# One visit instead of two for the softmax sums of the last head pair, at the seam between attention and a routed MLP

## The chip, the cores and the metric

The kernel runs on one core of one Trainium2 chip. The metric is the device time of one execution in microseconds (us), the median of three runs. A profiled execution of the same kernel gives the trace from which all durations below come.

## What is computed

The reference, cut to what matters. Attention in which a query sees only the keys of its own cluster, then a router that sends each token to one of eight experts:

```python
q_assign = argmax(q_n @ c_n.T)              # 16 clusters per head; k_assign likewise
mask = q_assign[..., :, None] == k_assign[..., None, :]
attn = softmax(where(mask, (q @ k.T) / 8, -1e9))        # B=4, H=8, S=768, D=64
x = (attn @ v).transpose(0, 2, 1, 3).reshape(3072, 512)
logits = unit(x) @ unit(expert_emb).T / tau              # 8 experts
expert_idx = argmax(logits); gate = softmax(logits)[expert_idx]
out[n] = gate[n] * (relu(x[n] @ w1[e]) @ w2[e])          # e = expert_idx[n], F=1024
```

Everything is float32.

## The kernel before

**Attention.** There are 16 pairs of heads, numbered n = 0 to 15: four to each batch, so that n = 12 to 15 make up batch 3. Each pair is cut into two groups of queries (hq = 0, 1; group g = 2n + hq) and each group into six tiles of 128 keys. One turn of the main loop (from L1547) treats two such units; a pair has turns it = 0 to 5, of which 0 to 2 belong to the first group and 3 to 5 to the second. In a turn TensorE (PE) makes the scores of the next turn (`scores`, L557), ScalarE (ACT) takes their exponentials (`expo`, L568), PE multiplies the previous ones with v (`attend`, L579), and VectorE (DVE) adds the exponentials up in `acc` (L588, L598).

**Dividing.** `total` (L617) sums `acc` over the partitions with a matmul against ones (L629). For an inner pair it is called once for both groups, one turn into the next pair: 8 matmuls of 32 x 192, then on DVE a transpose and a reciprocal of 12 values to a row (L646, L647), then eight small copies on GpSimd (POOL, L650) into `inv2`; two turns later `divide` (L654) spreads them by a DVE transpose (L661) and multiplies (L665). For the last pair it is called once for each group, each with 2 matmuls of 64 x 384 and a DVE reciprocal of 384 values to a row (L638): group 30 at turn 3, group 31 behind attention. `rows` (L676) transposes the result (L682) and writes it to the internal DRAM tensor x_rows (L689, four DMAs on the queue of SyncE, SP). `route_pieces` holds the router: `products` (L708) multiplies x with the expert vectors, in one visit for both groups of a batch or, in batch 3, once for each; `logits` (L720), `choose` (L756 to L763), `read` (L730, L735) and `norms` (L741) follow.

**The MLP.** The order of work on every engine is written out by hand; a scheduler reorders nothing, and each engine runs its queue in order. Four early items E0[0] to E0[3], each of 128 tokens of batches 0 and 1, are treated while the last routing is still being worked out. `spread_rows` sends their token numbers through DRAM (L1098, L1100), and `spread_pieces` turns them into addresses (two DVE instructions, L1106 and L1107). `early_lot(j, n)` issues the next n of the four indirect gathers of item j on POOL (L1130), optionally behind a copy of one element, `pace` (L1460), which makes POOL wait for a tile of ACT. `turn_x` transposes the gathered rows (L1248 on DVE; for E0[0] on PE, L1255, and ACT, L1258). `hidden` multiplies with w1 (L1372) in two halves of 512 columns, each followed by a relu on ACT (L1379); `result` multiplies with w2 (L1412) and ACT scales by the gate (L1423). `weights1` and `weights2` load 2 MB each on SP (L1180).

**The routing chain.** With all batches chosen, `pb.ranks` counts on PE (L844, L851). DVE then runs one long chain: `firsts`, `dest`, `hot_blocks` (L1007, L1011; L1010 on POOL) and `hot_rows` (L1017), after which PE makes `tokens` (L1026). `pieces` (L1115 on PE, L1123 on DVE) gives the addresses for the later items. From there PE alternates hidden and result of blocks and "sized" items (L1279, L1317) until the end.

Of the kernel before, what the change touches and what calls it, by code (L numbers as in the profile page):

```python
# [9 lines left out]
F32 = mybir.dt.float32  # L10
# [3 lines left out]
ACTF = mybir.ActivationFunctionType  # L14
AXX = mybir.AxisListType.X
EngineType = mybir.EngineType
PSUM = bass.MemoryType.PSUM

P = 128

SQ = 32
# [13 lines left out]
def bc(ap, shape, axis):  # L35
    return ap.unsqueeze(axis).to_broadcast(shape)
# [3 lines left out]
def kernel(  # L40
# [576 lines left out]
    def total(*gs):  # L617

        g = gs[0]
        d = gr[g]  # L620
        n = units[GU * g][0]
        G = len(gs)
        bk = misc()

        M, W = (D, HS) if G == 1 else (D // 2, HS // 2)
        for i in range(P // M):
            for k, g in enumerate(gs):
                c = i * W % HS
                nc.tensor.matmul(  # L629
                    bk[M * i : M * i + M, W * k : W * k + W],  # L630
                    lhsT=ones[:, 0:M],
                    rhs=gr[g]["acc"][:, i * W // HS, c : c + W],
                    start=True,
                    stop=True,
                )
        den = d["den"] = smp.tile([P, G, HS], F32, tag="den", name="den", bufs=1)
        if G == 1:
            nc.vector.reciprocal(den[:, 0], bk[:, 0:W])  # L638
            return


        U = W // SQ
        sums = smp.tile([P, G * U, SQ], F32, tag="sums", name="sums", bufs=1)
        inv = smp.tile([P, G, U], F32, tag="inv", name="inv", bufs=1)
        inv2 = d["inv2"] = smp.tile([P, G, 2, U], F32, tag="inv2", name="inv2", bufs=1)
        nc.vector.transpose(sums.rearrange("p g i -> p (g i)"), bk[:, 0 : G * W])  # L646
        nc.vector.reciprocal(inv.rearrange("p k u -> p (k u)"), sums[:, :, 0])  # L647
        for i in range(4):
            for to in (i, i ^ 1):
                nc.gpsimd.tensor_copy(  # L650
                    inv2[M * to : M * to + M, :, i % 2], inv[M * i : M * i + M]
                )

    def divide(*gs):  # L654
        n, hq, _ = units[GU * gs[0]]
        d = gr[gs[0]]
        G = len(gs)
        if hq == 0:
            xT[pairs[n]] = xp.tile([P, 2, HS], F32, tag="xT", name="xT", bufs=4)
        if G == 2:  # L660
            nc.vector.transpose(  # L661
                d["den"].rearrange("p k (u t) -> p (k u) t", t=SQ),
                bc(d["inv2"].rearrange("p k h u -> p (k h u)"), [P, G * HS // SQ, SQ], 2),
            )
        nc.vector.scalar_tensor_tensor(  # L665
            out=xT[pairs[n]][:, hq : hq + G],
            in0=ld[n]["o_sum"][:, hq : hq + G, 0:HS],
            scalar=ld[n]["o_sum"][:, hq, HS:HE],
            in1=d["den"],
            op0=ALU.add,  # L670
            op1=ALU.mult,
        )
        for g in gs:
            gr[g].clear()

    def rows(*gs):  # L676

        n, hq, _ = units[GU * gs[0]]
        b, hp = pairs[n]
        G = len(gs)  # L680
        xb = smp.tile([P, G * HS // SQ, SQ], F32, tag="xb", name="xb", bufs=2)
        nc.vector.transpose(  # L682
            xb.rearrange("p g i -> p (g i)"),
            xT[b, hp][:, hq : hq + G].rearrange("p k t -> p (k t)"),
        )
        t0 = S * b + HS * hq
        for c in range(P // SQ):
            c0 = P * c + SQ * hp
            nc.sync.dma_start(  # L689
                out=x_rows[t0 : t0 + G * HS, c0 : c0 + SQ].rearrange("(g t) i -> t g i", t=SQ),  # L690
                in_=xb[SQ * c : SQ * c + SQ],
            )
# [533 lines left out]
    def order_x(it):  # L1226

        d = mo[it]
        d["rows"] = xip.tile([P, KD, NQ, SQ], F32, tag="rows", name="rows")
        nc.gpsimd.tensor_copy(d["rows"], d["xin"].rearrange("p w (c i) -> p c w i", i=SQ))  # L1230
# [124 lines left out]
    def flat(t):  # L1355
        return t.rearrange("p k w -> p (k w)")

    def hidden(it, halves=(0, 1)):

        d = mo[it]  # L1360
        for half in halves:
            if half == 0:
                d["hT"] = (
                    flat(szp.tile([P, KF, max(CAPS)], F32, tag="hTs", name="hTs", bufs=1))[:, 0:F]
                    if it.kind == "whole"
                    else mop.tile([P, F], F32, tag="hT", name="hT")
                )
            f0 = 512 * half
            bk = psH.tile([P, 512], F32, tag="h_ps", name="h_ps")
            for m in range(0, 512, P):  # L1370
                for c in range(KD):
                    nc.tensor.matmul(  # L1372
                        bk[:, m : m + P],
                        lhsT=w1s[it.slot][:, c, f0 + m : f0 + m + P],
                        rhs=d["xT"][:, P * c : P * c + P],
                        start=(c == 0),
                        stop=(c == KD - 1),
                    )
            nc.scalar.activation(d["hT"][:, f0 : f0 + 512], bk, ACTF.Relu)  # L1379

    def result_last(it):

# [18 lines left out]
    def result(it, halves=(0, 1)):  # L1401
# [42 lines left out]
            pa.spread_rows(),  # L1444
        ),
        (3, 2, 3): lambda: fetch(E0[0]),
        (3, 2, 5): lambda: (order_x(E0[0]), pa.spread_pieces()),
        (3, 3, 2): lambda: early_lot(1, 2),
        (3, 3, 3): lambda: early_lot(1, 1),
        (3, 3, 4): lambda: early_lot(1, 1),  # L1450
# [94 lines left out]
    with tc.manual_schedule(engines=by_hand):  # L1545
        begin()
        for i in range(0, len(units), 2):  # L1547
            n, it = divmod(i // 2, NJ)

            if n == it == 0:  # L1550
                load(2, "qk")
            if it == 2 and n + 1 < NP:
                load(n + 1, "v")
            if it >= 4 and n + 3 < NP:
                load(n + 3, "qk"[it - 4])
            for m in range(i + 2 if i else 4, min(i + 4, len(units))):
                scores(m)
                expo(m)
                if it == 2 and m == i + 2:
                    piece(n + 1, "codes")  # L1560
            if (n, it) == (0, 1):
                piece(1, "products")
            between(n, it)
            if it == 4 and n == NP - 1:
                divide(2 * n)
            b, nb = divmod(n, NHP)
            if (b, nb, it) in early:
                early[b, nb, it]()
            if it >= 4:
                piece(n + 2, f"turn{it - 4}")  # L1570
            if i + 2 == len(units):
                ats.close()
                tile_waits = {"side": "right", "reuse_waits": "tile"}
                psX = ctx.enter_context(tc.tile_pool(name="psX", bufs=1, space=PSUM, **tile_waits))
                turn_x(E0[0], nc.scalar.copy, xp.tile([P, DM], F32, tag="acc", name="xTm", bufs=3))
            for m in range(i, i + 2):
                attend(m)
                if m == 0:
                    scores(3, (1,))
                    scores(3, (0,))  # L1580
                    expo(3)
            if it == 2:
                if n > 0:
                    divide(2 * n - 2, 2 * n - 1)
                unite(2 * n)
            elif it == 5:
                unite(2 * n + 1)
            if i + 2 == len(units):
                rows(ngroups - 2)
                route[b][0](0)  # L1590
            if it == 0 and n > 0:
                total(2 * n - 2, 2 * n - 1)
            if it == 0 and n > 0:
                piece(n + 1, "products")
            if (nb, it) == (0, 4) and b > 0:
                route[b - 1][0](0, 1)
            if it == 3 and n == NP - 1:
                total(2 * n)
        at.close()
        mop = ctx.enter_context(tc.tile_pool(name="mop", bufs=2, **tile_waits))  # L1600
        rtb = ctx.enter_context(tc.tile_pool(name="rtb", bufs=1, **tile_waits))
# [9 lines left out]
        gates = gate_pieces(0, B - 1)  # L1611
        gates[0]()
        early_lot(2, 1)
        logits(0)
        hidden(E0[0], (0,))
        turn_x(E0[1])
        early_lot(2, 2, mo[E0[0]]["hT"][0:1, 511:512])
        total(ngroups - 1)
        divide(ngroups - 1)
        ato.close()  # L1620
        psY = ctx.enter_context(tc.tile_pool(name="psY", bufs=1, space=PSUM, reuse_waits="tile"))
        rows(ngroups - 1)
        gates[1]()
        gates[2]()
        hidden(E0[0], (1,))
        turn_x(E0[2])
        gates[3]()
        early_lot(3, 2, mo[E0[0]]["hT"][0:1, F - 1 : F])
        weights1(E0[2])
        read(0, NJ, P - SQ, P)  # L1630
        products(1)
        hidden(E0[1], (0,))
        logits(1)
        choose()
        early_lot(3, 2, mo[E0[1]]["hT"][0:1, 511:512])
        hidden(E0[1], (1,))
        weights1(E0[3])
        pb.ranks()
# [8 lines left out]
        pb.hot_blocks()  # L1647
        pb.hot_rows(0, 1)
        hidden(E0[2])
        pb.experts()  # L1650
        weights1(later[0])
        result(E0[1], (0,))
# [186 lines left out]
```

## Time and profile before

| quantity | value |
|---|---|
| median of three runs | 695.13 us (694.39 to 695.2) |
| the profiled execution's own time | 691.63 us |
| its span, first to last instruction | 689.8 us |
| PE busy in the span | 680.6 us, 99% |
| DVE / POOL / ACT busy | 383.7 / 274.5 / 262.7 us |
| granted clock of PE | 0.998 |
| first router product behind attention (L708) | 323.69 us |
| first matmul of E0[3] | 362.94 us |

The profile is read as follows. A line of the timeline has the start in us from the start of the span, the length in us, the engine, the source line, the operation, what it writes and reads, the shape, and the count of merged instructions; brackets give the idle time of the engine before it and what ended it. A float32 matmul shows as two records. A busy PE says only that some matmul was in flight.

### The profile page before, as it was taken

Reading aid. Unit: us, or ns where it says so; the run is one execution under the profiler, and the core shown is the slowest. Engines: PE = TensorE matmul, PEld = TensorE weight load, DVE = VectorE, ACT = ScalarE, POOL = GpSimd, SP = SyncE. Lnnn points to the kernel's source line nnn. Section 1 sums busy time; section 2 is a strip of 40 time slices with the busy share of each in tenths; the row PEclk is TensorE's granted clock in tenths of the full one; section 3 lists DMA queues with packets and bytes.
Section 4 is the critical chain, followed back from the end, with each engine's and each line's share of the span. In section 5 each row is a group of like instructions: output and inputs, shape, how many; then the busy total and the mean of one; then the engine's idle time right before and its main releaser. Section 6 shows DMA issues by size and latency. Waiting matters only on the chain.

```text
span 689.8 us, 16335 instructions
## 1 busy us (share of the span) xinstructions
PE 680.6 (99%) x6521; PEld 459.6 (67%) x6521; DVE 383.7 (56%) x673; ACT 262.7 (38%) x444; POOL 274.5 (40%) x507
## 2 busy tenths in 40 slices
PE   8999999999999999999999999999999999999997
PEld 4444444444444444445866678888979797979795
DVE  6889898998889999979674122140210303030310
ACT  6666565577656765566242120101010111111011
POOL 3222221321132221326526343576746464647403
PEclk9999999999999999999999999999999999999999
DMA  9656665875677677789799967357777676878640
GB/s 152 118 81 113 106 98 85 161 143 102 107 132 158 114 153 159 182 204 255 205 323 395 354 221 271 120 201 281 287 244 284 213 288 249 304 257 305 234 169 34
DMA packets 244989, 135.55 MB, mean 196 GB/s; under 512 B 208673, under 2 KB 208675, under 8 KB 244909
## 3 DMA queue, kind: packets, MB, share of 16 engines
q1 hardware_dynamic: 237740, 121.09, 65.6%
q0 software_dynamic: 6224, 13.14, 5.6%
q8 instruction: 53, 0.87, 0.5%
q10 hardware_dynamic: 944, 0.23, 0.1%
q14 instruction: 28, 0.22, 0.1%
HBM read 115.93 MB, written 13.12 MB: 187 GB/s over the span
## 4 chain that ended last, share of the span: by engine, by line
PE 80%; DVE 7%; issue 5%; DMA 5%; POOL 1%; ACT 1%; POOLq 0%; SPq 0%; DVEq 0%; ACTq 0%
PE s_ps L557 17%; PE o_ps L579 14%; PE h_ps L1372 10%; PE y_ps L1412 10%; PE h_ps L1279 9%; PE y_ps L1317 6%; PE misc L1317 5%; PE x_ps L1279 3%; DVE acc L598 3%; DMA out_dram<-ys,spidx 2%; PE misc L629 2%; DMA w1s<-in_moe_w_dram 1%; PE misc L418 1%; PE misc L708 1%; POOL out_dram L1141 1%
## 5 line engine op out<-in xcount | busy, mean ns | idle before, releaser
L568 ACT ACTIVATE prob<-s_ps 128x768 f32<-128x768 f32 x192 | 154.4, 814 | 102.1 <-PE s_ps L557 101.2
L557 PE MATMUL s_ps<-qT,kT 64*64 64x384 f32 x1536 | 156.0, 483 | 0.0
L579 PE MATMUL o_ps<-prob,v 64*64 64x385 f32 x1536 | 141.2, 484 | 0.0
L598 DVE TENSOR_TENSOR acc<-acc,prob 128x768 f32<-128x768 f32 x128 | 121.3, 948 | 8.8 <-ACT prob L568 0.5
L579 PEld LDWEIGHTS o_ps<-prob,v 64*64 64x64 f32 x1536 | 58.1, 133 | 64.8 <-issue 56.8
L1326 DVE STREAM_TRANSPOSE ys<-y_ps 128x256 f32<-128x256 f32 (+4 forms) x16 | 6.5, 412 | 147.7 <-PE y_ps L1317 147.7
L1372 PEld LDWEIGHTS h_ps<-xTm,w1s 128*128 128x128 f32 x768 | 87.3, 192 | 2.0 <-issue 1.5
L1372 PE MATMUL h_ps<-xTm,w1s 128*128 128x128 f32 x768 | 88.3, 276 | 0.0
L557 PEld LDWEIGHTS s_ps<-qT,kT 64*64 64x64 f32 x1536 | 55.3, 133 | 36.3 <-issue 32.4
L1412 PE MATMUL y_ps<-w2s,hT 128*128 128x512 f32 x176 | 77.8, 594 | 0.4 <-PEq L1720 0.4
L613 POOL COPY behind<-acc 1x1 f32<-1x1 f32 x30 | 6.7, 222 | 172.3 <-DVE acc L598 167.9
L1279 PE MATMUL h_ps<-xTs,w1s 128*128 128x272 f32 (+7 forms) x384 | 72.8, 346 | 0.0
L1279 PEld LDWEIGHTS h_ps<-xTs,w1s 128*128 128x128 f32 x384 | 66.7, 190 | 6.6 <-issue 2.9
L1141 POOL DMA_INDIRECT out_dram<-ys,spidx x56 | 56.2, 1004 | 36.4 <-issue 20.0
L1379 ACT ACTIVATE hT<-h_ps 128x512 f32<-128x512 f32 x24 | 14.3, 596 | 143.7 <-PE h_ps L1372 143.6
L557 PE MATMUL s_ps<-hot 64*64 64x384 bf16 x768 | 64.4, 325 | 0.6 <-ACT hot L511 0.6
L1130 POOL DMA_INDIRECT xs<-x_rows,gpidx x56 | 56.9, 1017 | 18.1 <-issue 17.2
L1412 PEld LDWEIGHTS y_ps<-w2s,hT 128*128 128x128 f32 x176 | 32.5, 190 | 37.5 <-issue 37.5
L557 PEld LDWEIGHTS <-hot 64*64 64x64 bf16 x768 | 23.9, 106 | 43.1 <-issue 41.2
L1317 PE MATMUL y_ps<-hTs,w2o 128*128 128x272 f32 (+7 forms) x256 | 48.0, 346 | 0.0
L1317 PE MATMUL misc<-hTs,w2o 128*128 128x272 f32 (+7 forms) x256 | 48.0, 346 | 0.0
L1317 PEld LDWEIGHTS y_ps<-hTs,w2o 128*128 128x128 f32 x256 | 44.4, 190 | 2.5
(288 smaller groups left out, 728.7 us busy)
## 6 DMA issues: line engine op xcount, KB each, us to landing
w1s<-in_moe_w_dram SPq DMA_DIRECT2D x18, 2048.0 KB, 8.6
w2s<-in_moe_w_dram SPq DMA_DIRECT2D x18, 2048.0 KB, 10.0
q<-in_q_dram SPq DMA_DIRECT2D x63, 96.0 KB, 3.9
k<-in_k_dram SPq DMA_DIRECT2D x63, 96.0 KB, 3.5
v<-in_v_dram SPq DMA_DIRECT2D x120, 48.0 KB, 2.1
x_rows<-xb SPq DMA_DIRECT2D x60, 96.0 KB, 2.7
xr<-x_rows SPq DMA_DIRECT2D x9, 512.0 KB, 4.5
w1s<-in_moe_w_dram SPq DMA_DIRECT2D x4, 1024.0 KB
```

What stands on the lines that cost most here:

```text
L557: nc.tensor.matmul(s_ps[D * half : D * half + D, h, 0:HS], lhsT=l[rows, half], rhs=r[rows], start=part == (1 if len(parts) < 2 else 0), st ...
L568: nc.scalar.activation(d["prob"][:, :, 0:HS], d["s_ps"][:, :, 0:HS], ACTF.Exp, scale=scale)
L579: nc.tensor.matmul(g["o_ps"][D * h : D * h + D, half, 0:HE], lhsT=ld[n]["v"][keys, j, h], rhs=d["prob"][keys, h, 0:HE], start=(j == 0), st ...
L598: nc.vector.tensor_tensor(g["acc"], g["acc"], d["prob"][:, :, 0:HS], ALU.add)
L629: nc.tensor.matmul(bk[M * i : M * i + M, W * k : W * k + W], lhsT=ones[:, 0:M], rhs=gr[g]["acc"][:, i * W // HS, c : c + W], start=True, s ...
L1130: nc.gpsimd.indirect_dma_start(out=to, out_offset=None, in_=of, in_offset=bass.IndirectOffsetOnAxis(ap=at, axis=0), bounds_check=n - 1, oo ...
L1141: inst = nc.gpsimd.indirect_dma_start(out=to, out_offset=bass.IndirectOffsetOnAxis(ap=at, axis=0), in_=of, in_offset=None, bounds_check=n - 1,
L1279: nc.tensor.matmul(bk, lhsT=w1s[it.slot][:, c, P * f : P * f + P], rhs=d["xT"][:, c, 0:C], start=(c == 0), stop=(c == KD - 1),)
L1317: nc.tensor.matmul(bks[g][:, 0:C], lhsT=d["w2"][:, f, P * g : P * g + P], rhs=d["hT"][:, f, 0:C], start=(f == 0), stop=(f == KF - 1),)
L1372: nc.tensor.matmul(bk[:, m : m + P], lhsT=w1s[it.slot][:, c, f0 + m : f0 + m + P], rhs=d["xT"][:, P * c : P * c + P], start=(c == 0), stop ...
L1379: nc.scalar.activation(d["hT"][:, f0 : f0 + 512], bk, ACTF.Relu)
L1412: nc.tensor.matmul(bk, lhsT=d["hT"][:, P * c : P * c + P], rhs=w2s[it.slot][:, c], start=(c == 0), stop=(c == KF - 1),)
```

## The change

Three things are edited, and the order of the seam with them.

1. `total` and `divide` lose their one-group form. The calls for group 30 at turns 3 and 4 of pair 15 go; groups 30 and 31 are summed, divided and written together behind attention. The router's products of batch 3 are likewise made in one visit (`products(0, 1)`), set between two quarters of E0[1]'s hidden layer: `hidden` gets a `span` for that.
2. `spread_pieces` moves from turn 5 of pair 14 to turn 1 of pair 15.
3. Behind attention, E0[1]'s transpose, the gate steps of the first three batches (`gates[1]` to `gates[3]`) and the load of w1 for E0[2] move ahead of the divide and of the x_rows writes; E0[2]'s transpose moves behind `choose`; the gathers of E0[3] move: one stays early, two are paced by the first half of E0[2]'s hidden layer and the last by its second half.

```diff
         (3, 2, 3): lambda: fetch(E0[0]),
-        (3, 2, 5): lambda: (order_x(E0[0]), pa.spread_pieces()),
+        (3, 2, 5): lambda: order_x(E0[0]),
+        (3, 3, 1): pa.spread_pieces,
...
-            if it == 4 and n == NP - 1:
-                divide(2 * n)
...
-            if i + 2 == len(units):
-                rows(ngroups - 2)
-                route[b][0](0)
...
-            if it == 3 and n == NP - 1:
-                total(2 * n)
...
         early_lot(2, 1)
-        logits(0)
+        turn_x(E0[1])
         hidden(E0[0], (0,))
-        turn_x(E0[1])
-        early_lot(2, 2, mo[E0[0]]["hT"][0:1, 511:512])
-        total(ngroups - 1)
-        divide(ngroups - 1)
-        ato.close()
-        psY = ctx.enter_context(tc.tile_pool(name="psY", bufs=1, space=PSUM, reuse_waits="tile"))
-        rows(ngroups - 1)
+        total(ngroups - 2, ngroups - 1)
         gates[1]()
         gates[2]()
         hidden(E0[0], (1,))
+        gates[3]()
+        weights1(E0[2])
+        divide(ngroups - 2, ngroups - 1)
+        ato.close()
+        psY = ctx.enter_context(tc.tile_pool(name="psY", bufs=1, space=PSUM, reuse_waits="tile"))
+        rows(ngroups - 2, ngroups - 1)
+        read(0, NJ, P - SQ, P)
+        hidden(E0[1], (0,), (0, 256))
+        products(0, 1)
+        hidden(E0[1], (0,), (256, 512))
+        early_lot(2, 2, mo[E0[0]]["hT"][0:1, F - 1 : F])
+        early_lot(3, 1)
+        logits(0, 1)
+        choose()
         turn_x(E0[2])
-        gates[3]()
-        early_lot(3, 2, mo[E0[0]]["hT"][0:1, F - 1 : F])
-        weights1(E0[2])
-        read(0, NJ, P - SQ, P)
-        products(1)
-        hidden(E0[1], (0,))
-        logits(1)
-        choose()
-        early_lot(3, 2, mo[E0[1]]["hT"][0:1, 511:512])
         hidden(E0[1], (1,))
...
         pb.hot_blocks()
         pb.hot_rows(0, 1)
         hidden(E0[2])
+        early_lot(3, 2, mo[E0[2]]["hT"][0:1, 511:512])
+        early_lot(3, 1, mo[E0[2]]["hT"][0:1, F - 1 : F])
         pb.experts()
```

More of the change, by code (lines that the diff above doesn't have):

```diff
@@ L623, in total @@
         bk = misc()
-        M, W = (D, HS) if G == 1 else (D // 2, HS // 2)
+        M, W = D // 2, HS // 2
         for i in range(P // M):
@@ L635, in total @@
                 )
[L636 to L639, printed above, removed]
+        d["den"] = smp.tile([P, G, HS], F32, tag="den", name="den", bufs=1)
         U = W // SQ
@@ L659, in divide @@
             xT[pairs[n]] = xp.tile([P, 2, HS], F32, tag="xT", name="xT", bufs=4)
[L660 to L664, printed above, removed]
+        nc.vector.transpose(
+            d["den"].rearrange("p k (u t) -> p (k u) t", t=SQ),
+            bc(d["inv2"].rearrange("p k h u -> p (k h u)"), [P, G * HS // SQ, SQ], 2),
+        )
         nc.vector.scalar_tensor_tensor(
@@ L1356, in flat, with hidden @@
         return t.rearrange("p k w -> p (k w)")
-    def hidden(it, halves=(0, 1)):
+    def hidden(it, halves=(0, 1), span=(0, 512)):
         d = mo[it]
         for half in halves:
-            if half == 0:
+            if half == 0 and span[0] == 0:
                 d["hT"] = (
@@ L1368, in hidden @@
             f0 = 512 * half
-            bk = psH.tile([P, 512], F32, tag="h_ps", name="h_ps")
-            for m in range(0, 512, P):
+            if span[0] == 0:
+                d["h_ps"] = psH.tile([P, 512], F32, tag="h_ps", name="h_ps")
+            bk = d["h_ps"]
+            for m in range(*span, P):
                 for c in range(KD):
@@ L1378, in hidden @@
                     )
-            nc.scalar.activation(d["hT"][:, f0 : f0 + 512], bk, ACTF.Relu)
+            if span[1] == 512:
+                nc.scalar.activation(d["hT"][:, f0 : f0 + 512], bk, ACTF.Relu)
     def result_last(it):
```

## The prediction

> **What bounds the kernel.** I read first the busy times, then what PE waited for, then the chain of waits before its one wait.
>
> ```profile
> PE 680.6 (99%) x6521; PEld 459.6 (67%) x6521; DVE 383.7 (56%) x673; ACT 262.7 (38%) x444; POOL 274.5 (40%) x507
> ```
>
> ```profile
> PE misc L629 <- DVE acc L598: 1.1, 1, 1.1
> ```
>
> ```profile
> 302.08 3.55 DMA early_f<-early_rows
> ...
> 305.75 0.25 DVE early_f L1106
> ...
> 308.17 0.88 PE misc L629 x14
> ```
>
> PE is the bound, with one wait of over 0.6 us behind the start: at turn 0 of pair 15 L629 needs group 29's `acc`, DVE holds that back behind L1106, and L1106 waits for the token numbers' DMA. A PE microsecond saved near here counts, unless something else then holds PE. So I priced the PE instructions from start to next start:
>
> ```profile
> 182.17 1.51 PE L708 MATMUL misc<-xT,embT 128*32 128x192 f32 x32
> 183.61 0.36 PE L557 MATMUL s_ps<-hot 64*64 64x384 bf16 x4
> ```
>
> ```profile
> 306.54 0.51 PE L629 MATMUL misc<-acc,ones 128*32 128x192 f32 x2
> 308.17 0.88 PE L629 MATMUL misc<-acc,ones 128*32 128x192 f32 x14 [1.12 <-DVE acc L598]
> 308.98 0.36 PE L557 MATMUL s_ps<-hot 64*64 64x384 bf16 x4
> ```
>
> ```profile
> 328.26 0.87 PE L629 MATMUL misc<-acc,ones 128*64 128x384 f32 x4
> 329.06 3.84 PE L1372 MATMUL h_ps<-xTm,w1s 128*128 128x128 f32 x32
> 332.82 0.87 PE L708 MATMUL misc<-xT,embT 128*32 128x96 f32 x32
> ```
>
> A products visit over both groups takes 1.44 us (182.17 to 183.61); one over half of them 0.80 (332.82 to 333.62, where the next line starts). A single-group total takes 0.80. Last, the engines that decide when the moved gathers go out:
>
> ```profile
> 310.89 4.30 POOL L650 COPY inv<-inv 32x12 f32<-32x12 f32 x8 [1.64 <-DVE inv L647]
> ```
>
> ```profile
> 352.07 4.23 DVE L1017 TENSOR_TENSOR ohrb<-io_b,lob 128x3072 bf16<-128x3072 bf16 x1
> ```
>
> ```profile
> 496.83 1.23 DVE L1341 TENSOR_TENSOR ys<-ys,gates 128x1024 f32<-128x1024 f32 x1
> ```
>
> ```profile
> 496.98 1.96 POOL L1130 DMA_INDIRECT xin<-x_rows,gpidx  x1 [0.30 <-issue]
> ```
>
> Eight L650 copies take 2.23 us at 290.13, but 4.30 here, beside four of DVE's acc additions. The gather at 496.98 takes 1.96 us instead of about 1.0; it ends 0.9 us after L1341 does.
>
> [...] every other copy there (0.80 to 0.82 us, the rest 0.18) ends just behind an addition, and a one-element L613 copy at 25.21 took 0.85 us under such an instruction, 0.18 elsewhere. [...] from issue to landing a gather took 3.0 us in a lull (331.07), 5.6 and 5.8 beside the weight loads (367.97, 369.32), at worst 7.9 (386.36).
>
> **Part by part.**
>
> *`spread_pieces` one turn later.* It issues two DVE instructions and no DMA. Its DMA had landed by 305.65; at the new place, behind L647 (about 308.3), it waits for nothing, and the gathers that need it follow on POOL behind the L650 copies, as before. DVE then ends group 29's `acc` near 304.7, before PE asks at 306.54. PE spent 308.98 - 306.54 = 2.44 us; the sixteen records alone cost 0.68 (286.92 to 287.60, where a like shape follows) to 0.90; I take 0.78. Gain 1.66.
>
> *Group 30's total gone from turn 3.* From `attend` to the next scores: 316.43 to 318.62 = 2.19 us, against 1.30 in the turn before (313.52 to 314.82). Gain 0.89.
>
> *First products gone.* 322.24 to 324.49 = 2.25, against 1.40 for an `attend` followed by a change of shape (320.26 to 321.66). Gain 0.85.
>
> *Joint total*: 0.77 for 0.80. Gain 0.03. *Joint products*: 1.44 for 0.80. Loss 0.64.
>
> PE sum: 1.66 + 0.89 + 0.85 + 0.03 - 0.64 = 2.79 us, bounds 2.5 to 2.95. L844 moves from 340.87 to 338.08.
>
> *New PE wait: the joint products' last four matmuls need pair 15's quotient.* Total ends 325.6; L647's successor 326.5; eight copies 2.23, since DVE has little here: 328.9; transpose and multiply 0.97 + 1.02: 331.0. PE arrives at 332.2. Cost nothing; with the 4.30 us of the row above, 0.7 us. The moved gate steps on DVE (eight small instructions) lie beside the copies. E0[1]'s transpose now stands ahead of the total's transpose and waits for four gathers, issued by about 318, so landed by 324: nothing. Two reciprocals of 2.55 us leave DVE, which isn't the bound: nothing.
>
> *SP.* Eight x_rows DMAs of 48 KB become four of 96 KB and fall behind gate_rows and w1 of E0[2]. That load goes out near 331.8 instead of 338.79 and takes 8.8 us; PE needs it at 345.3 (348.10 - 2.79), so the old 338.79 + 8.8 = 347.6 would have become a stall, and it doesn't. x_rows and the reads behind queue after it and pass about when they did; w1 of E0[3] follows near 347 (was 348.37).
>
> *E0[2]'s transpose ahead of the routing chain.* Its last gather goes out near 332.6 and lands in 5 us beside that load; transposed by 338.4, when L859 is due. Delay of DVE's chain 0 to 0.8; I take 0.15. So L1017 ends at 356.30 - 2.79 + 0.15 = 353.66.
>
> *E0[3]'s gathers: the added wait that decides.* Before, they went out by 341.2. Now three of them stand behind the four gate gathers, a scatter and L1010. POOL takes a `pace` copy when L1010 is done, about 350.4[...]: it ends at 353.7. Queued behind it: gather (1.03), pause 0.31, gather (1.00), the second `pace` (relu done by 353.1), pauses of 0.16: the last gather is issued at 356.6. The DMA engines are then full, w1 and w2 loads of 4 MB from 347 on and the next from 356: 5.5 us to landing, 362.1. DVE transposes in 0.71, with L1123 queued behind: PE can begin E0[3] at 362.9. PE is ready at 362.94 - 2.79 = 360.15. Stall 2.75 us, bounds: nothing (landing within 3.5) to 5.1 (7.9).
>
> From there PE runs as before, from 362.9 against 362.94. All later loads wait for PE or for addresses that come when they came.
>
> **Sum.** -2.79 + 2.75 = about 0. The profiled execution took 691.63 (span 689.8 and 1.8 around it) and lies 3.5 below the median, 695.13; a difference in microseconds carries over. Forecast 695.1; its own range, 694.0 to 696.3, from landings of 4.5 to 6.5. A change of 0.2%, 1.4 us, is about what a measurement of this kernel can tell from none.
>
> **Rivals.**
>
> *The gain stays (0.28).* If POOL's `pace` copy gets in ahead of L1017, the last gather goes out with the relu, near 353.9, lands at 359.4, is turned by 360.2: no stall, 692.3. A landing of 4.1 gives half: 693.7. For it: the first half's relu is done by 349.6, well before L1017 ends, and some gathers needed only 3.0. Against: L1010 stands ahead in POOL's queue[...]; the weights fill the engines.
>
> *Slower (0.14).* The same gather lands late: with 7.9, PE begins E0[3] at 365.3, 2.4 us later than now: 697.5. It decides from a landing of 6.9 us on (stall 4.2). For it: 6.6 to 7.9 stand in the trace. Against: those were the first of their burst, and this is the last.
>
> *The quotient comes late.* Stall of 0.7 at the joint products, which pushes the routing chain as much: 695.8, inside the likeliest case.
>
> *The old stall doesn't go*: L1106's wait would only move. Against: its DMA landed 2.6 us before the new place.
>
> **Chances.** No change 0.58, faster by over 0.2% 0.28, slower 0.14. The range 692.4 to 696.8 leaves out the full gain's lower edge and the late landing, some 0.15.
>
> **What would show it.** Right: no PE wait at L629 at 306.5, L844 near 338.1, one new PE wait of 2 to 3.5 us before L1372 of E0[3], released by DVE's transpose, itself by the gather; a `pace` copy of some 3 us beside L1017. Wrong: that copy at 0.18 us; a last gather before 355; a wait at L708; or L844 later than 338.6.

## The result, and the profile after

| runs of one session | before, us | after, us | after / before (95% interval) |
|---|---|---|---|
| the result | 695.04 (22 runs) | 697.88 (22 runs) | 1.0035 (1.0023 to 1.0047) |
| chip 3 | 691.03 (33) | 696.66 (2) | 1.008 (1.0062 to 1.0099) |
| chip 7 | 695.30 (39) | 700.36 (21) | 1.0062 (1.0048 to 1.0075) |

The change makes the kernel slower: by 2.8 us of the median in the result, by 5.1 to 5.6 in two later sessions. The forecast was 695.1, no change. Chips differ in their base: the kernel before takes a median of 690.9 to 691.0 us on two of them and 695.0 to 695.3 in the other sessions. Medians are set against those of the kernel before from the same session; where profiles of different sessions are compared, the text says so.

The page's busy times after, and the list of what PE waited for (total, times, longest):

```profile
PE 682.8 (98%) x6497; PEld 462.5 (66%) x6497; DVE 379.9 (54%) x671; ACT 262.6 (38%) x444; POOL 283.6 (41%) x515
```

```profile
PE h_ps L1369 <- issue: 4.3, 1, 4.3
PE idle_ps L235 <- DVE epsc L258: 1.1, 1, 1.1
PE h_ps L1274 <- ACT hTs L1281: 0.9, 1, 0.9
```

The wait for `acc` is gone from the list and a wait of 4.3 us ahead of E0[3] is new ("issue": the profile names nothing that PE waited for; DVE's transpose of E0[3]'s rows, shown below, ends 0.1 us before PE goes on). (Lines of the changed kernel are 2 to 5 lower: L1372 is L1369 now, L708 is L703, L844 is L839, L1017 is L1012, L1130 is L1125.) PE's timeline of the changed kernel, the seam and then E0[3]:

```profile
326.61 0.88 PE L629 MATMUL misc<-acc,ones 128*32 128x192 f32 x16
...
332.97 1.51 PE L703 MATMUL misc<-xT,embT 128*32 128x192 f32 x32
...
339.87 0.25 PE L839 MATMUL misc<-cumx,onesb 128*128 128x200 bf16 x1
...
361.73 0.28 PE L1110 MATMUL misc<-tkb22b,identb 128*32 128x44 bf16 x16
366.31 9.73 PE L1369 MATMUL h_ps<-xTm,w1s 128*128 128x128 f32 x64 [4.29 <-issue]
375.88 2.31 PE L1410 MATMUL y_ps<-w2s,hT 128*128 128x512 f32 x5
```

One total and one products visit, as intended. The end of this stretch in the kernel before:

```profile
362.94 7.41 PE L1372 MATMUL h_ps<-xTm,w1s 128*128 128x128 f32 x64
370.19 2.31 PE L1412 MATMUL y_ps<-w2s,hT 128*128 128x512 f32 x5
```

So there are two losses, not one: the wait of 4.29, and behind it 64 records that take 375.88 - 366.31 = 9.57 us where the kernel before took 370.19 - 362.94 = 7.25. Why the second, tells the table by stretches of the changed kernel (length; busy time and instructions of PE, its weight loads, DVE, ACT and POOL; then the granted clock, the DMA share and GB/s):

```profile
362.00:364.00 2.00, 0.01 (x4) 0.00 (x0) 0.00 (x0) 1.81 (x2) 1.02 (x1) 1.00 1.02 403
364.00:366.00 2.00, 0.00 (x0) 0.00 (x0) 0.51 (x1) 0.00 (x0) 0.00 (x0) 0.60 1.00 367
366.00:368.00 2.00, 1.69 (x8) 1.72 (x9) 1.83 (x9) 0.00 (x0) 0.00 (x0) 0.50 0.99 285
368.00:370.00 2.00, 2.00 (x11) 2.00 (x11) 1.49 (x10) 0.24 (x1) 1.55 (x2) 0.50 1.05 412
370.00:372.00 2.00, 2.00 (x15) 2.00 (x14) 1.79 (x9) 0.00 (x0) 1.48 (x2) 0.69 1.05 403
```

While PE stood idle, its granted clock fell to 0.5, and it stayed there until 371.2, for 6.8 us; 11 records fit into 2 us instead of 20. What PE waited for shows on DVE and then POOL (changed kernel):

```profile
340.73 0.71 DVE L1243 STREAM_TRANSPOSE xTm<-xin 128x512 f32<-128x512 f32 x1 [2.51 <-DMA xin<-x_rows,early_i]
341.37 0.33 DVE L854 COPY rkb<-misc 128x200 f32<-128x200 f32 x1
...
351.91 4.23 DVE L1012 TENSOR_TENSOR ohrb<-io_b,lob 128x3072 bf16<-128x3072 bf16 x1
...
365.50 0.71 DVE L1243 STREAM_TRANSPOSE xTm<-xin 128x512 f32<-128x512 f32 x1 [4.68 <-DMA xin<-x_rows,early_i]
```

```profile
352.88 3.30 POOL L1459 COPY pace<-hT 1x1 f32<-1x1 f32 x1
356.34 1.10 POOL L1125 DMA_INDIRECT xin<-x_rows,early_i  x1 [0.16 <-ACT junk L736]
357.75 1.00 POOL L1125 DMA_INDIRECT xin<-x_rows,early_i  x1 [0.31 <-issue]
358.76 0.18 POOL L1459 COPY pace<-hT 1x1 f32<-1x1 f32 x1
359.09 1.03 POOL L1125 DMA_INDIRECT xin<-x_rows,early_i  x1 [0.16 <-issue]
```

In the kernel before, the last of these gathers went out 18 us earlier:

```profile
341.20 0.99 POOL L1130 DMA_INDIRECT xin<-x_rows,early_i  x1 [0.31 <-issue]
```

The place and the chain are those of the prediction: the `pace` copy under L1012, the gathers behind it, the transpose behind the last landing. Its sizes are not.

### The profile page after: what moved, and what is told of

Its sections match the earlier page's. It is cut to its first block, busy times and chain, and to the rows that moved or that the text cites. A ratio compares the mean times of both kernels' runs of the same rounds, so it can differ in the third digit from the quotient of the medians.

```text
span 697.0 us, 16296 instructions
## 1 busy us (share of the span) xinstructions
PE 682.8 (98%) x6497; PEld 462.5 (66%) x6497; DVE 379.9 (54%) x671; ACT 262.6 (38%) x444; POOL 283.6 (41%) x515
## 5 line engine op out<-in xcount | busy, mean ns | idle before, releaser
L1369 PE MATMUL h_ps<-xTm,w1s 128*128 128x128 f32 x768 | 90.6, 280 | 4.3 <-issue 4.3
L1369 PEld LDWEIGHTS h_ps<-xTm,w1s 128*128 128x128 f32 x768 | 89.7, 196 | 6.6 <-issue 6.5
L1125 POOL DMA_INDIRECT xs<-x_rows,gpidx x56 | 56.9, 1017 | 18.9 <-issue 18.9
L646 POOL COPY inv<-inv 32x12 f32<-32x12 f32 x128 | 33.0, 258 | 42.2 <-DVE inv L643 32.0
```

The source lines that it names most:

```text
L646: nc.gpsimd.tensor_copy(inv2[M * to : M * to + M, :, i % 2], inv[M * i : M * i + M])
L1125: nc.gpsimd.indirect_dma_start(out=to, out_offset=None, in_=of, in_offset=bass.IndirectOffsetOnAxis(ap=at, axis=0), bounds_check=n - 1, oo ...
L1369: nc.tensor.matmul(bk[:, m : m + P], lhsT=w1s[it.slot][:, c, f0 + m : f0 + m + P], rhs=d["xT"][:, P * c : P * c + P], start=(c == 0), stop ...
```

## The experiments

The theory after the result: E0[3]'s late gathers cost about 6.6 us (4.3 of waiting, and 2.3 of half clock behind it), and the saving on PE stands beside that. The rivals: the reordered seam loses time by itself (loads on SP, transposes on DVE), or the half clock is given back later.

**1. The gathers early** (changed kernel; two runs, on two chips).

```diff
         choose()
+        early_lot(3, 3)
         turn_x(E0[2])
...
         hidden(E0[2])
-        early_lot(3, 2, mo[E0[2]]["hT"][0:1, 511:512])
-        early_lot(3, 1, mo[E0[2]]["hT"][0:1, F - 1 : F])
```

> The changed kernel, with the three remaining gathers of E0[3] issued right behind the second batch's choice, without pace. Theory 1 (the loss is the late last gather of E0[3]: a PE wait of 4.3 us and, behind it, 64 matmuls that took 9.6 instead of 7.2 us at half clock): the last gather goes out near 343 to 346 instead of 359.1, PE has no wait ahead of E0[3]'s first product, the granted clock stays at 1.0, and the 2.8 us saved on PE stay: about 692.3, range 691.5 to 693.5. Theory 2 (the reordered seam itself costs: the loads' order on SP or the routing chain that came 1 us later on DVE): PE loses the same time elsewhere, 697 to 698. In between, 694 to 695, if the early gathers push E0[2]'s load or transpose.

> The version with E0[3]'s gathers right behind the choice once more, beside the others on this chip, as the candidate that beats both kernels. If the seam's saving (1.7 us in the second pair of profiles) stays: 1.2 to 1.8 us below before. If the early gathers push E0[2]'s load or the second layer of E0[0]: 0 to 0.8 below.

Measured: 694.06 against 695.14 before, ratio 0.9981 (0.9964 to 0.9997); the second time 689.53 against 690.94, ratio 0.9983 (0.9976 to 0.9989). In the second profile three gathers start between 337.46 and 340.09, and PE goes on at once:

```profile
360.41 0.28 PE L1110 MATMUL misc<-tkb22b,identb 128*32 128x44 bf16 x16
360.62 7.41 PE L1369 MATMUL h_ps<-xTm,w1s 128*128 128x128 f32 x64
```

So the seam doesn't lose by itself, and this version beats both kernels, by 1.1 to 1.4 us against before. The first expectation's 692.3 was too low. The profile of that run shows a second place where a saving is lost: PE waits 2.03 us for a relu near 660, and the clock is at half again behind it:

```profile
660.00:662.00 2.00, 2.00 (x10) 2.00 (x9) 0.00 (x0) 0.36 (x2) 0.53 (x1) 0.50 1.09 404
662.00:664.00 2.00, 2.00 (x11) 2.00 (x11) 0.00 (x0) 0.30 (x1) 0.00 (x0) 0.65 0.35 133
```

**2. The late gathers alone** (kernel before).

```diff
-        early_lot(3, 2, mo[E0[0]]["hT"][0:1, F - 1 : F])
+        early_lot(3, 1, mo[E0[0]]["hT"][0:1, F - 1 : F])
...
-        early_lot(3, 2, mo[E0[1]]["hT"][0:1, 511:512])
...
         hidden(E0[2])
+        early_lot(3, 2, mo[E0[2]]["hT"][0:1, 511:512])
+        early_lot(3, 1, mo[E0[2]]["hT"][0:1, F - 1 : F])
```

> The kernel before, with only E0[3]'s last three gathers moved to where the changed kernel has them: behind E0[2]'s first layer, two of them paced by its first half, the last by its second. Everything else of the change is left out. Theory 1 (this one move makes the loss): POOL's pace copy stands beside L1017 for 3.3 us, the last gather goes out near 358, lands 6 us later, PE waits 2.5 to 4 us ahead of E0[3], and[...] the clock at half adds 2: 2.5 to 6 us slower than before. Theory 2 (the loss needs the reordered seam, its SP queue or DVE queue): less than 1 us slower.

Measured: 696.51 against 690.94, 5.6 us slower, ratio 1.0085 (1.0071 to 1.0099). This one move alone costs as much as the whole change does on a base of 691, in a kernel that has nothing else of it:

```profile
365.09 9.01 PE L1372 MATMUL h_ps<-xTm,w1s 128*128 128x128 f32 x64 [3.23 <-issue]
373.94 4.46 PE L1412 MATMUL y_ps<-w2s,hT 128*128 128x512 f32 x10
```

A wait of 3.23 us was enough for a half clock, though a shorter one (3.4 us against 6.8): 373.94 - 365.09 = 8.85 us for the 64 records, 1.6 over the 7.25 of full speed. (The profiled execution, 695.32, was the fastest of the five.) In the changed kernel the same gathers lose more, about 7.0 us by the profiles of experiment 8 on that base: 4.99 of waiting and 2.05 of clock, with 1.67 of saving against it.

**3. L1012 in short pieces** (changed kernel; a small cast of `lo` to float32 feeds it).

```diff
+            if self.part == 1:
+                for u in range(n):
+                    nc.vector.tensor_scalar(
+                        self.oh[:, u], io_b, self.lo32[:, u : u + 1], None, ALU.is_equal
+                    )
+                return
```

> The changed kernel, with the 4.23 us DVE instruction at L1012 (two SBUF operands) made as 24 tensor_scalar instructions of one SBUF tensor each, plus one small cast. Theory 1[...]: the pace copy takes 0.2 to 0.5 us instead of 3.3, the last gather goes out 1.5 to 3 us earlier, PE's wait falls to 1.5 to 2.8 us, the clock stays full, 693.5 to 695.5. Theory 2 (the copy waits for something else, or landing alone decides): the copy still takes 3 us and more, 697 to 698. If the 24 instructions together take over 6 us, PE waits for them at L1021 and the gain is lost there.

Measured: 690.33 against 691.03 (0.9999, 0.9989 to 1.0009; three of the 21 runs took 2.6 to 5.4 us more than the median, so the ratio is nearer to 1 than the medians are). The changed kernel took 696.66 in the same session, in two runs: 6.3 us given back. DVE and POOL of this kernel:

```profile
350.83 4.83 DVE L1017 TENSOR_SCALAR ohrb<-io_b,lo32b 128x128 bf16<-128x128 bf16 x24
360.29 0.71 DVE L1252 STREAM_TRANSPOSE xTm<-xin 128x512 f32<-128x512 f32 x1 [2.73 <-DMA xin<-x_rows,early_i]
```

```profile
351.79 0.18 POOL L1468 COPY pace<-hT 1x1 f32<-1x1 f32 x1
352.12 1.11 POOL L1134 DMA_INDIRECT xin<-x_rows,early_i  x1 [0.16 <-issue]
...
354.94 1.03 POOL L1134 DMA_INDIRECT xin<-x_rows,early_i  x1 [0.16 <-issue]
```

The copy takes 0.18 instead of 3.3 us while DVE is just as busy (4.83 us), so what held it was the form of the DVE instruction. The run changes two things of that form at once, two SBUF tensors to one and one long instruction to 24 short ones; which of them frees the copy was not separated. The last gather goes out 3.0 us earlier than in the second profile of the changed kernel (experiment 8), it lands in 5.3 us instead of 6.5, and PE waits 0.73. With the gathers where the change put them, this kernel is no slower than the one before once the copy isn't held.

**4. The wait filled** (changed kernel; 14 matmuls whose results nothing uses).

```diff
+        keep_up(14, misc())
         hidden(E0[3])
```

> The changed kernel, with 14 matmuls of 128x512 bf16 (some 3.2 us at 0.23 us each, results unused) ahead of E0[3]'s first product, where PE waited 4.3 us. The gather comes no earlier. Theory 1 (the wait costs twice: itself, and the clock granted at half for 6.8 us behind it): the wait shrinks to about 1 us, the clock stays at 1.0, the 64 matmuls behind take 7.2 us again, and the time falls by 2.4 us to about 695.5. Theory 2 (the half clock is absorbed by a later wait): no change, 697.5 to 698.2. If the fill reaches past the gather's landing it costs up to 0.5 us more.

> The kernel with 14 filling matmuls ahead of E0[3] once more, since its first run had the routing chain 2.5 us later than the changed kernel's, which hid what the fill does. Theory 1 (the half clock costs 2.1 to 2.4 us on top of the wait): if L1012 starts near 351 as in the changed kernel, E0[3] starts where it did there, its 64 matmuls take 7.2 us instead of 9.3, and the time is 1.8 to 2.4 us below the changed kernel's, which was 5.6 above the kernel before on one chip and 2.8 on the other. Theory 2 (the clock's loss is given back): no gain.

Measured: the first run 698.79 against 695.14 (1.005, 1.0032 to 1.0068), which looks like theory 2. Its profile says why it tells nothing: E0[2]'s gather landed late, so L1012 began at 354.37 instead of 351.91 and E0[3] at 368.77. The second run, with L1012 at 350.01: 693.95 against 690.94 (1.0056, 1.0042 to 1.007), 3.0 above before, where the changed kernel was 5.6 above on a chip of equal base.

```profile
360.29 3.20 PE L235 MATMUL misc<-onesb 128*128 128x512 bf16 x14
364.45 7.38 PE L1369 MATMUL h_ps<-xTm,w1s 128*128 128x128 f32 x64 [0.96 <-issue]
371.67 6.60 PE L1410 MATMUL y_ps<-w2s,hT 128*128 128x512 f32 x15
```

E0[3] begins 0.84 earlier than in the second profile of the changed kernel (365.29, on the other chip), and its records take 7.22 instead of 9.30 (374.59 - 365.29). The two profiled executions differ by 3.0 us (693.42 and 696.42), and these two terms make 2.9 of them, 2.1 by the clock, which stayed at 1.00 here. It isn't given back.

**5. The loads held back** (changed kernel; a small DMA that reads E0[3]'s transposed tokens stands ahead of the two loads on SP).

```diff
-        weights2(E0[2])
...
-        weights1(later[0])
...
         turn_x(E0[3])
+        nc.sync.dma_start(out=early_rows[0:1, 0:1], in_=mo[E0[3]]["xT"][0:1, DM - 1 : DM])
+        weights2(E0[2])
+        weights1(later[0])
```

> The changed kernel, with the second-layer load of E0[2] and the first-layer load of the first later item held on SP until E0[3]'s tokens are transposed. Theory 1 (the last gather takes 6.4 us because it shares the DMA engines with these loads): it lands in 3 to 4 us, PE's wait ahead of E0[3] falls from 4.3 to 1 to 2 us, the clock stays full, 693.5 to 695, unless the held load is then late for E0[2]'s second layer, needed near 370.6. Theory 2 (the landing doesn't come from the loads): the wait stays near 4.3 us and the time is 697.5 or more.

Measured: 703.70 against 695.14 (1.0114, 1.0088 to 1.0139). The held load then came too late, as feared. What was asked is answered all the same: the last gather, issued at 359.84, had landed by 362.5, in 2.7 us instead of 6.4. From 356 to 360 us the DMA engines were 0.07 busy and from 360 to 364 us 0.12, against 1.05 and 1.01 in the changed kernel.

```profile
362.52 0.71 DVE L1243 STREAM_TRANSPOSE xTm<-xin 128x512 f32<-128x512 f32 x1 [3.69 <-DMA xin<-x_rows,early_i]
```

```profile
363.33 7.38 PE L1369 MATMUL h_ps<-xTm,w1s 128*128 128x128 f32 x64 [1.11 <-issue]
373.37 8.83 PE L1410 MATMUL y_ps<-w2s,hT 128*128 128x512 f32 x16 [2.65 <-DMA w2s<-in_moe_w_dram]
```

**6. E0[2]'s transpose later** (changed kernel).

```diff
         choose()
-        turn_x(E0[2])
...
         pb.firsts()
+        turn_x(E0[2])
```

> The changed kernel, with E0[2]'s transpose on DVE moved behind the routing steps pb.ranks and pb.firsts. Theory 1 (part of E0[3]'s lateness is DVE's queue: the transpose, waiting for E0[2]'s gather, holds the routing chain back by 1.1 us and more, so L1012 and the paced gathers behind it come late): L1012 ends by 354.9 instead of 356.1, the last gather goes out near 357.9 instead of 359.1, PE's wait falls to 2.5 to 3.3 us and the clock stays full: 694.5 to 696.5. Theory 2 (only landing and the loads decide when E0[3]'s tokens come): 697.3 to 698.3.

Measured: 695.95 against 691.03 (1.0065, 1.0051 to 1.0079), 0.7 below the changed kernel in that session. Routing follows the counts at once (`rkb` at 338.74 instead of 340.11), and L1012 begins at 350.10 instead of 350.74. Less of that arrived than expected: the last gather went out at 357.29, landed in 6.5 us again, and PE's 3.60 us of waiting still halved the clock, for 6.8 us. The wait is 1.3 shorter than in the changed kernel's profile of that session, but the 64 records behind it take 374.60 - 364.64 = 9.96 us instead of 9.30, so half of the gain is lost to the clock. The order on DVE is one small term.

**7. The spread step alone** (kernel before).

```diff
-        (3, 2, 5): lambda: (order_x(E0[0]), pa.spread_pieces()),
+        (3, 2, 5): lambda: order_x(E0[0]),
+        (3, 3, 1): pa.spread_pieces,
```

> The kernel before, with the spread addresses' last step one turn later and nothing else. Theory 1 (the stall at the group total of pair 15's turn 0 goes, and nothing else is late): that wait of 1.1 us is gone, the two instructions span 0.8 instead of 2.4 us, about 693.4, range 692.9 to 693.9. Theory 2 (what PE gains there is lost at E0[2]'s weight load, issued at 338.79 and needed at 348.1, or at a gather of the early items): 694.8 to 695.3.

> The kernel before with only the spread addresses' last step moved, once more. On the chip of its first run, whose base was 695, it gained nothing, but exponentials on ScalarE came up to 4.5 us late there. If the chip is one with a base of 691: 0.5 to 0.8 us below before (the saving at L629 was 0.61 in the second pair of profiles). If the stall of L629 only moves: 0 within 0.2.

Measured: 695.64 against 695.14 (1.0013, 1.0 to 1.0025), then 690.52 against 690.94 (0.9996, 0.9988 to 1.0004). It gives 0.4 us at best, on the one chip, which is not clear of the noise, and nothing on the other.

**8. Both kernels again.** The first profile of before was 3.5 us under its median, and those of the experiments on a base of 695 showed odd stalls.

> The kernel before, unchanged, for a second profile on the chip and in the session of the experiments. Its first profile lasted 691.63 us, 3.5 below its median. Theory 1 (what the experiments show between 314 and 322 us, exponentials on ScalarE 1 to 4 us late and PE behind them, and a PE wait for the relu near 660 us, comes of the edits): the second profile shows neither, and its L844 comes near 340.9. Theory 2 (both belong to an ordinary execution, and the first profile was one without them): it shows both, L844 comes 2 to 3 us later, near 343.5, and the time is about 695.

> The changed kernel, unchanged, for a second profile. The PE wait ahead of E0[3] should be 3.5 to 5 us again, behind a last gather issued between 358 and 361, with the clock at half for 6.8 us behind it[...]; 697 to 699. If the wait is below 2 us here and the time still 697 to 698, the wait isn't what costs.

> The kernel before, unchanged. If its time is near 695: theory 1 (exponentials on ScalarE come late and PE behind them between 314 and 322 us, as in the four experiments on that chip, and PE waits for a relu near 660) shows 2.5 to 3.5 us of lateness by L844 or E0[2] and 1 to 3 near 660; theory 2 (the time lies outside, or is spread over the span) shows none at these places. If its time is near 691, the chip is not that one and the question stays open.

> The changed kernel, unchanged, beside it. Near a base of 691: 5 to 6 us slower than before, with a PE wait of 4 to 5 us ahead of E0[3] and the 64 matmuls behind it over 9 us. Near a base of 695: 2.5 to 3.2 us slower.

Measured: b0 690.82, a0 696.66 (base 691); b1 695.29, a1 700.36 (base 695). The kernel before has two faces. On the base of 695 two exponentials on ScalarE come late, and much later PE waits for a relu; the profile on the base of 691 has neither. ScalarE and then PE, from b1:

```profile
317.96 0.62 ACT L741 ACTIVATE junk<-xr 128x512 f32<-128x512 f32 x1
318.49 0.19 ACT L741 ACTIVATION_READ_ACCUMULATOR junk<-xr 128x1 f32 x1
322.52 0.81 ACT L568 ACTIVATE prob<-s_ps 128x768 f32<-128x768 f32 x1 [3.84 <-remote]
```

```profile
342.90 0.25 PE L844 MATMUL misc<-cumx,onesb 128*128 128x200 bf16 x1
...
364.98 7.41 PE L1372 MATMUL h_ps<-xTm,w1s 128*128 128x128 f32 x64
372.22 4.03 PE L1412 MATMUL y_ps<-w2s,hT 128*128 128x512 f32 x9
```

```profile
661.39 3.53 PE L1279 MATMUL h_ps<-xTs,w1s 128*128 128x160 f32 x24 [1.55 <-ACT hTs L1286]
```

So theory 2 of b0's expectation holds for such chips. It also means that the prediction's profile, which has neither of the two stalls and so looks like base 691, and the three times beside it (base 695) didn't belong together. After and before are best compared by profiles of equal base. The pair on 691 is of one session and chip:

```profile
361.97 7.41 PE L1372 MATMUL h_ps<-xTm,w1s 128*128 128x128 f32 x64
369.22 7.03 PE L1412 MATMUL y_ps<-w2s,hT 128*128 128x512 f32 x16
```

```profile
365.29 9.46 PE L1369 MATMUL h_ps<-xTm,w1s 128*128 128x128 f32 x64 [4.92 <-issue]
374.59 3.60 PE L1410 MATMUL y_ps<-w2s,hT 128*128 128x512 f32 x8
```

The first two lines are b0's, the others a0's. In the table, the pair on 695 is of two sessions:

| us, after minus before | forecast | base 695: result against b1 | base 691: a0 against b0 |
|---|---|---|---|
| counts on PE (L839, L844) | -2.79 | 339.87 - 342.90 = -3.03 | 338.23 - 339.90 = -1.67 |
| first product of E0[3] | 0.0 | 366.31 - 364.98 = +1.33 | 365.29 - 361.97 = +3.32 |
| its second layer | 0.0 | 375.88 - 372.22 = +3.66 | 374.59 - 369.22 = +5.37 |
| time of the profiled runs | 0 | 698.80 - 695.42 = +3.38 | 696.42 - 690.67 = +5.75 |

The +3.66 on the base of 695 is made up of -3.03 up to the counts, +4.36 of waiting and +2.33 of half clock. Of it 0.63 goes back at the wait near 660 that both have (1.55 in b1, 0.92 in the result's profile). That leaves 3.0 of the 3.38 between the profiled runs; between the medians of the result it was 2.84.

## Why the prediction was wrong

**The saving on PE was right in its parts but one.** 2.79 was forecast; on the base of 691 it is 1.67. The largest part, 1.66 for the stall at L629, was read from one execution that waited 1.12 us there. In b0 PE is held there for less, which leaves 0.61 to gain, and experiment 7, which moves this step alone, gained nothing clear of the noise. With 0.61 for 1.66 the forecast would be 1.74. On the base of the times the counts come 3.03 earlier, but some 1.1 of that are the late exponentials, which held PE longer in b1 than in the result's profile, so its nearness to 2.79 is in part luck. Group 30's total (0.90 for 0.89) and the first products (0.80 for 0.85) came out, and so did the joint visits (a loss of 0.66 for 0.61).

**"Stall 2.75 us" is the step that failed**, together with the full clock taken for granted behind it. The stall was 4.29 in the result's profile and 4.92 in a0. Two of its terms were too small.
- *"I take 0.15" for DVE's chain.* E0[2]'s transpose stands ahead of the routing steps, and it was not done "by 338.4": the last gather landed at 340.7 (339.5 in a0). Before, `rkb` followed L844 by 0.37 us; now it follows L839 by 1.50 (result) and 1.88 (a0). So the delay was 1.1 and 1.5, beyond the bound of 0.8; at L1012's end 0.7 and 1.2 more than the forecast's 0.15 were left. E0[2]'s last gather went out at 332.73 in a0 (334.37 in the result's profile), near the forecast's 332.6; but it took 6.7 and 6.4 us beside that load, not 5.
- *"5.5 us to landing".* It took 6.4 and 6.5. Experiment 5 shows that the loads make it: 2.7 with two of them held back.

Together the two terms give 2.75 + 0.7 + 0.9 = 4.3 for the result and 2.75 + 1.2 + 1.0 = 4.9 for a0, which is what was measured. The chain between was right: the copy under L1012, which experiment 3 frees (that it ends with that instruction was my estimate; it ended at 356.18, L1012 at 356.14), and from L1012's end to the last issue 2.94 forecast, 359.09 - 356.14 = 2.95 measured. The lower bound was not: by the same sum a landing of 3.5 leaves a stall of 0.75, and only one of 2.75 leaves none.

**A term was missing.** "From there PE runs as before" took an idle PE for one that resumes at full speed. I didn't ask what the stall of my own sum, 2.75 with a bound of 5.1, would do to the clock. In the traces of these runs every stretch at half clock ahead of the kernel's last 4 us lasted 3.4 us, behind waits of 2.03, 2.13, 2.65 and 3.23, or 6.8, behind waits of 3.60, 4.29, 4.92 and 5.05. Waits of 0.73 to 1.66, one of 2.49 and one of 2.64 left it at full. The stall as forecast lies between the 2.65 and the 3.23 that halved the clock. So even it was near a jump of 1.6 to 2.7 us, while the range was drawn as if the loss grew evenly with the landing, and ended at 696.8.

**The rival "slower" named the right place**: a late last gather of E0[3]. Its 697.5, from a landing of 7.9, was near the measured 697.88, but that is luck: the landing was 6.4, and the rest came of the late chain and of the clock. Its 0.14 was too little: E0[2]'s landing, E0[3]'s landing and the held copy all had to be as short as taken for the sum to be zero, and each had more room above than below.

**What the forecast of no change hid.** Its two halves, -2.8 and +2.8, were of different kinds: a saving of instructions, and a wait on transfers with a wide spread. Undoing only the second (experiment 1) gives the version that is faster than both kernels.

## What to carry to other kernels

A step moved later "because there is time" has to be followed to its last transfer, with each queue ahead of it at its late bound, before the saving is counted. In these traces PE waits of 2.03, 2.13 and 2.65 us halved the clock behind them and two of 2.49 and 2.64 did not; each of the five of over 3 (3.23 to 5.05) cost twice: itself, and 1.6 to 2.7 us of half clock. Fourteen filling matmuls took away the second part (7.22 us for the 64 records instead of 9.30); the cure is an earlier issue. The `pace` copy ahead of the gathers took 3.30 us beside L1012 and 0.18 beside the 24 instructions of experiment 3. Place such gathers ahead of the long instruction, as experiment 1 did, or write it as short ones with one tensor and a scalar for each partition, as experiment 3 did.

## What was unexpected

- The clock's fall isn't decided by the wait's length alone: 2.03 us were enough once, near 660; 2.49 were not, in experiment 4's first run, nor were 2.64 in experiment 5, whose wait of 2.65 had been enough 11 us earlier. What tells them apart was not shown: no experiment moved such a wait by itself.
- Twenty-four `tensor_scalar` instructions took 4.83 us for what one `tensor_tensor` did in 4.23, and a POOL copy beside them 0.18 instead of 3.3.
- The same kernel takes 691.0 us on two chips and 695.3 on others, and the gap sits in two places, 2.1 us between 318 and 324 and 1.8 near 660 in b1 against b0, with 0.7 before. Why ScalarE's exponentials come late there (their wait ends in an event that the trace doesn't name) was not settled.
- On the base of 695 the change cost 2.8 us in one session and 5.1 in another (chip 7). The a1 profile, 704.56, lies 4 us over its own median, but 2.9 of them are lost long ahead of anything that the change touches: PE's first L629 comes at 37.70 instead of 34.80 in b1. With these taken out, a1 against b1, of one session, has the counts 2.2 us earlier, E0[3] 2.9 later and its second layer 5.2 later, about the 5.1 between the medians and much like the pair on the base of 691. Why the result's session lost less stays open; its one profile waited 4.29 instead of 5.05 ahead of E0[3], and 0.92 instead of 1.66 near 660.
